# A RetNet attention stage and a PReLU MLP in one kernel: the first part's decays moved into its mask, into k and into q's copy, other unread products on the matrix engine, and another order of creation

## The chip, the cores and the metric

The kernel runs on one core of a Trainium2 chip. The time is that of the device in microseconds (us), the median over several executions; lower is better. Besides, one execution was taken by the hardware profiler, and everything that is read out of a profile or a trace below comes from that one execution.

The engines are named as the profile names them: PE multiplies matrices (PEld is its loading of the stationary operand), DVE and ACT work elementwise and read the accumulators, POOL works elementwise but not on the accumulators, SP issues the transfers (DMA).

## What is computed

```python
def _attn_ref(q, k, v):                      # 8 x 8 heads x 576 x 64 each
    scores = scale * np.matmul(q, k.transpose(0, 1, 3, 2))
    gamma = 1.0 - 2.0 ** (-5.0 - np.arange(H))
    rel = pos[:, None] - pos[None, :]
    Dmat = np.where(rel >= 0, gamma[:, None, None] ** rel[None, :, :], 0.0)
    return np.matmul(scores * Dmat, v)

def _moe_ref(x, w_in, w_out, alpha):         # x: 4608 x 512, d_ff 2048
    h = x @ w_in
    g = np.maximum(h, 0.0) + alpha * np.minimum(h, 0.0)
    return g @ w_out
```

x is the attention's output, with the 8 heads of a token side by side. All inputs and the output are float32.

## The kernel before

**Attention in chunks.** The 576 positions of a head are 9 chunks of 64. Within a chunk the scores are masked and multiplied into v; from chunk to chunk a state (k transposed times v, with its decay) is carried. For the first two batches this is done in six *parts* (`PARTS`): part x is batch x // 3, and chunks 0-3, 4-7 or 8, for all heads at once. `load_part` loads k, q and v of a part (256 KB each time that it is called for one m, two m per tensor); `part_transposes(x, i)` turns k (i = 0) or q (i = 1) on PE and ACT copies it out; `part_scale(x, i)` multiplies q (i = 1) or v (i = 2) on POOL by a table of decays `tp`, so that the decay between two positions comes out of the product of two factors; `part_scores`, `part_states` and `part_values` are the products of 64 x 64; the scores are masked on DVE, `part_carry` hands the state on by POOL; ACT copies the result into x. `last_part` does parts 2 and 5 (one chunk). Later batches go through `joint`, two heads at a time, whose operands come by their own loads (`load_kq`, `load_kn`, `load_v`), by `operands` and by round trips through DMA.

**The MLP.** The 4608 tokens are 18 blocks of 256. Eight `cells`, a block with two of the sixteen slices of d_ff each, are done first and plainly (`unit_plain` makes h, `second_plain` multiplies by w_out); they use the weights as 32 pieces, loaded and rebuilt one by one by `weights` / `convert`: two operations on ACT, three on DVE, one on POOL (L754), in this order. One piece is 512 KB. Cell 0 (block 0, slice 0) needs pieces 0 and 1 for its two halves of `unit_plain` and 2 and 3 for the two products of each half m of `second_plain`; cell 1 (block 0, slice 1) needs 4 and 5, then 6 and 7. Everything after that goes with operands split into three parts (`split_w`, `split_roll`, `unit_roll`, `second`).

**What sets the order.** Every operation is recorded with `do(engine, cost, function, reads, writes)`; the creation order decides which operation waits for which when they share a buffer, and which bank of the accumulators each gets. Then `dues` and `plan` put all recorded operations in an order by a table of costs written in the kernel, a random search changes the due times, and the order with the smallest planned total is written out. So each engine gets one fixed sequence, and it executes that sequence in order: an instruction that waits holds up all those behind it on its engine. Loads all go through SP's queue; in the first part of the run a load waits until at most 1.25 MB are under way (`IN_FLIGHT`). `fill(n, cost)` records n products of 128 x 128 that nothing reads (18 in all: 5, 3 and 10). `tables` makes small tables of decays, on DVE (L393 to L403).

**The first steps** stand at the end of the function: loads of part 0, `fill(5)`, k's transposes, `fill(3)`, q scaled and transposed, the scores, v scaled, three pieces of weights, the states, `tables`, the values, `fill(10)`, then part 1 between the cells, and so on up to `split_w`; then a loop over s makes the rest.

Of the kernel before, what the change touches and what calls it, by code (L numbers as in the profile page):

```python
# [10 lines left out]
FP32 = mybir.dt.float32  # L11
# [6 lines left out]
ALU = mybir.AluOpType  # L18
# [3 lines left out]
def kernel(  # L22
# [120 lines left out]

    gch = const.tile([P, 3, NPAIR], FP32, name="gch")
# [34 lines left out]
    def do(eng, cost, fn, r=(), w=(), late=0.0, lock=False, kind=None, hold=0.0, size=0):  # L179
# [19 lines left out]
        op.deps = [d for d in deps if d is not op]  # L199
# [145 lines left out]
    EARLY, JOINTS = 1, {(s, i): 1 for s in range(14) for i in range(2) if (s, i) not in ((0, 0), (8, 1), (10, 1), (13, 0), (13, 1))}  # L345
# [46 lines left out]
    def tables():  # L392
        nc.vector.reciprocal(pf[:, 1], pf[:, 1])  # L393
        nc.vector.tensor_tensor(out=th[:, 1], in0=pf[:, 1], in1=th[:, 2], op=ALU.mult)
        for h2 in range(2):
            hd = slice(h2 * D, (h2 + 1) * D)
            nc.vector.tensor_copy(tabk[half(1 - h2)], th[half(1 - h2), 1, h2:H:2])
            nc.vector.tensor_copy(gch[hd, 0], th[hd, 2, h2:H:2])
            nc.vector.tensor_scalar(tabx[hd, :, 0], pf[hd, 0, h2:H:2], QSCALE, None, ALU.mult)
            nc.vector.scalar_tensor_tensor(out=tabx[hd, :, 1], in0=dif[hd, 5, h2:H:2], scalar=1.0,  # L400
                                           in1=tabx[hd, :, 0], op0=ALU.add, op1=ALU.mult)
        for i in range(2):
            ins = nc.vector.tensor_tensor(out=gch[:, i + 1], in0=gch[:, i], in1=gch[:, i],  # L403
                                          op=ALU.mult)
        return ins


# [41 lines left out]
    def part_scale(x, i):  # L449
        j0, j1 = PARTS[x % 3]  # L450
        rows = min(P, (j1 - j0) * C)
        for m in range((j1 - j0 + 1) // 2):
            def f(m=m):
                t = part(x, i)[0:rows, m]
                return nc.gpsimd.tensor_tensor(
                    out=t, in0=t, in1=tp[0:rows, i - 1, m, :, None].to_broadcast([rows, H, D]),
                    op=ALU.mult)
            do("POOL", 1.05, f, (), [key_p(x, i, m)], lock=True)
# [8 lines left out]
    def part_transposes(x, i, bank):  # L467
# [6 lines left out]
        for m in range(2):  # L474
# [9 lines left out]
            def g(m=m, pt=pt):  # L484
                nc.scalar.copy(at()[:, :, m * P:(m + 1) * P],
                               pt.get().rearrange("p (c s) -> p c s", c=NPAIR))
            do("ACT", 0.59, g, [(pt, 0)], [(t, "t", m)])

    def part_scores(x, bank):
# [18 lines left out]
        for h2 in range(2):  # L508
            def g(h2=h2):
# [3 lines left out]
                    in1=mask[:, None, :].to_broadcast([P, 8, C]), op=ALU.mult)  # L513
            do("DVE", 0.69, g, [(ps[h2], 0), (ps[h2], 1)], [(a, "m", h2)])
# [892 lines left out]

    def of_pe():
        return [op for op in ops if op.eng == "PE"][-1:]

    load_part(0, ((0, 0), (1, 0), (1, 1), (0, 1), (2, 0), (2, 1)))
    bank = banks_of(0)
    fill(5, 0.43)
    part_transposes(0, 0, bank)
    fill(3, 0.43, [next(op for op in ops if op.eng == "PE" and len(op.deps))])
    part_scale(0, 1)
    part_transposes(0, 1, bank)
    part_scores(0, bank)
    part_scale(0, 2)
    weights(3)  # L1420
    part_states(0, bank)
    do("DVE", 2.0, tables, (), [(cst, "t")])
    part_carry(0)
    part_values(0, bank)
    fill(10, 0.25, of_pe())
    weights(1)
    fetch_x(visits[0])
    dma(lambda: a16, lambda: moe_alpha.rearrange("(t p) -> t p", p=P), NFC * P * 4, (), [(cst, "al")])
    aps = Gen(psa[0])
    do("PE", 0.2, lambda: nc.tensor.transpose(aps.get()[:, 0:NFC], a16, ident[0:NFC, 0:NFC]), [(cst, "al")],  # L1430
       [(aps, 0)])
    do("DVE", 0.1, lambda: nc.vector.tensor_scalar(malpha, aps.get()[:, 0:NFC], -1.0, 1.0,
                                                   ALU.mult, ALU.add), [(aps, 0)], [(cst, "a")])
    load_part(1)
    bank = banks_of(1)
    unit_plain(cells[0])
    weights(2)
    part_transposes(1, 0, bank)
    part_scale(1, 1)
    part_transposes(1, 1, bank)  # L1440
    second_plain(cells[0])
    weights(2)
    part_scale(1, 2)
    part_scores(1, bank)
    part_states(1, bank)
    unit_plain(cells[1])
    load_part(2)
    part_values(1, bank)
    part_carry(1)
    fetch_x(visits[1])  # L1450
    part_scale(2, 1)
    part_scale(2, 2)
    rooms(3)
    load_part(3)
    second_plain(cells[1])
    unit_plain(cells[2])
    last_part(2)
    weights(2)
    for x in (4, 5):
        rooms(x)  # L1460
    part_transposes(3, 0, bank)
    part_scale(3, 1)
    part_transposes(3, 1, bank)
    second_plain(cells[2])
    part_scores(3, bank)
    part_scale(3, 2)
    part_states(3, bank)
    part_carry(3)
    unit_plain(cells[3])
    part_values(3, bank)  # L1470
    load_part(4)
    weights(2)
    second_plain(cells[3])
    part_transposes(4, 0, bank)
    part_scale(4, 1)
    part_transposes(4, 1, bank)
    unit_plain(cells[4])
    load_part(5)
    weights(2)
    second_plain(cells[4])  # L1480
    part_scores(4, bank)
    part_scale(4, 2)
    part_states(4, bank)
    part_carry(4)
    unit_plain(cells[5])
    part_values(4, bank)
    load_kq(8)
    load_kn(8)
    load_v(8)
    weights(2)  # L1490
    second_plain(cells[5])
    part_scale(5, 1)
    part_scale(5, 2)
    unit_plain(cells[6])
    last_part(5)
    operands(8)
    load_kq(9)
    load_v(9)
    second_plain(cells[6])
    unit_plain(cells[7])  # L1500
    done.add(8)
    joint_(8)
    second_plain(cells[7])
    for i in range(16):
        split_w(i)

    ready_kb = [((kb + 1) * TB - 1) // S for kb in range(NKB)]
    todo = iter(range(2 * NPAIR + 1, len(pairs) + 1))
# [103 lines left out]
    was_in = lxs[0].gen.ops + lxs[1].gen.ops  # L1612
    lxs[:] = lx_slots("x")
    for x in lxs:
        Gen(x).before = was_in
    for _ in range(EARLY):
        joint_(next(todo))
    land[0] = LAND[1]
    split_roll(visits[2])
    last = singles - 1  # L1620
    t = 8
    for s in range(last):
# [3 lines left out]
        queue += [now_cells[vis["n"], u] for vis in some for u in us]  # L1626
        quick[0] = s >= QUICK
        by_side = sorted(some, key=lambda vis: vis["kb"] % 2)
        if s == 0:
            split_roll(visits[3])  # L1630
        for i, u in enumerate(us):
            cs = [now_cells[vis["n"], u] for vis in by_side]
            gens, g = take_rooms(cs)
            for f in range(2):
                for _ in range(ahead.get(t, 0)):
                    convert((op_, 0), was, None)
                t += 1
                ps = unit_roll(by_side, u, f, True)
                acts_roll(ps, gens, g, u, f)
                if f:  # L1640
                    for c, ga in zip(cs, gens):
                        c["ga"] = ga, ga.get
                    ahead_g()
# [104 lines left out]
```

## Time and profile before

| | us |
|---|---|
| median of 3 runs | 919.32 |
| lowest and highest of them | 918.11, 922.28 |
| profiled execution, its span | 917.4 |
| PE busy in it | 906.9 (99%) |
| DVE, ACT, POOL busy | 548.0, 503.9, 520.2 |

The span is the time from the first to the last instruction; the median of the runs lies 1.9 us above the span of the profiled execution. A row of the timeline gives start, duration, engine, line, operation, output and inputs, shapes, how many instructions are drawn together, and in brackets the engine's idle time before it with what ended it. "issue" stands where nothing in the profile is seen to have been waited for. A matmul's end is modelled, so a row can reach a little into the next one.

### The profile page before, as it was taken

What the parts mean: (1) busy time and instruction counts of PE and PEld (TensorE: products, weight loads), DVE (VectorE), ACT (ScalarE), POOL (GpSimd) and SP (SyncE); (2) the same over time, 40 slices, a digit from 0 to 9 for tenths busy, and PEclk for the clock granted to TensorE, in tenths of its full rate; (3) what the DMA queues carried; (4) which work ended last, traced back from release to release, by engine and by line L of the source; (5) the groups of instructions that cost most, each with busy time, mean ns of one, the idle gap of its engine ahead of it and who ended that gap; (6) DMA issues with size and microseconds to landing.
All of it is one profiled execution on the core that took longest, in us unless ns stands there. A gap on an engine that the chain in (4) does not pass through costs nothing. (4 is left out here: it accounts for less than half of the span.)

```text
span 917.4 us, 19097 instructions
## 1 busy us (share of the span) xinstructions
PE 906.9 (99%) x7289; PEld 737.8 (80%) x7289; DVE 548.0 (60%) x1003; ACT 503.9 (55%) x1010; POOL 520.2 (57%) x461
## 2 busy tenths in 40 slices
PE   7999999999999999999999999999999999999998
PEld 6767688887888888888888888888888888888886
DVE  5786766667677667676757776344444534344343
ACT  4575455646565656565746555537463636364441
POOL 4776746456466665674542244665656656574624
PEclk9999999999999999999999999999999999999999
DMA  9995688977988879895243332212121322211112
GB/s 216 251 235 86 164 189 186 198 178 155 221 192 194 209 166 201 193 189 181 93 138 130 102 125 65 86 57 81 58 89 56 99 73 86 74 64 47 47 46 69
DMA packets 235947, 121.32 MB, mean 132 GB/s; under 512 B 203456, under 2 KB 203728, under 8 KB 235856
## 3 DMA queue, kind: packets, MB, share of 16 engines
q1 hardware_dynamic: 235712, 119.98, 52.1%
q8 instruction: 57, 0.93, 0.4%
q14 instruction: 34, 0.28, 0.1%
q10 hardware_dynamic: 144, 0.13, 0.0%
HBM read 74.19 MB, written 32.51 MB: 116 GB/s over the span
## 5 line engine op out<-in xcount | busy, mean ns | idle before, releaser
L1340 PE MATMUL pso<-w,g 128*128 128x512 f32 x1392 | 338.8, 391 | 0.0
L1340 PEld LDWEIGHTS pso<-w,g 128*128 128x128 f32 x1392 | 258.9, 188 | 55.2 <-POOL g L1267 1.2
L1264 POOL TENSOR_TENSOR g<-ga_all,g 128x512 fp32r<-128x512 f32 x76 | 97.9, 1291 | 130.4 <-ACT g L1260 105.0
L1267 POOL TENSOR_TENSOR g<-g 128x512 fp32r<-128x512 f32 x114 | 147.4, 1294 | 23.7 <-DVE su L1066 5.7
L1188 PE MATMUL psh<-lx_x,w 128*128 128x512 f32 (+1 forms) x360 | 86.6, 379 | 0.0
L1188 PE MATMUL psa<-lx_x,w 128*128 128x512 f32 (+1 forms) x360 | 85.4, 376 | 0.0
L1188 PEld LDWEIGHTS psa<-lx_x,w 128*128 128x128 f32 x360 | 65.1, 188 | 13.1 <-issue 0.4
L1188 PEld LDWEIGHTS psh<-lx_x,w 128*128 128x128 f32 x360 | 64.2, 188 | 12.9
L1260 ACT ACTIVATE g<-ga_all 128x512 fp32r<-128x512 f32 x76 | 47.6, 631 | 43.0 <-PE pso L1340 21.0
L1256 POOL TENSOR_TENSOR g<-g 128x512 fp32r<-128x512 f32 x22 | 28.5, 1296 | 64.0 <-DVE g L1253 38.3
L1264 POOL TENSOR_TENSOR g<-vn,g 128x512 fp32r<-128x512 f32 x25 | 32.4, 1297 | 37.5 <-ACT g L1260 34.9
L1340 PE MATMUL pso<-lx_x,g 128*128 128x512 f32 x216 | 53.5, 390 | 0.1
L1163 POOL TENSOR_TENSOR lx_x<-lx_x 128x512 fp32r<-128x512 f32 x28 | 35.9, 1294 | 26.0 <-DVE lx_x L1160 26.0
L941 DVE SCALAR_TENSOR_TENSOR at<-psa,pf,mask 64x512 f32<-64x512 f32 x48 | 36.0, 749 | 21.1 <-PE psh L861 10.2
L1340 PEld LDWEIGHTS pso<-lx_x,g 128*128 128x128 f32 x216 | 40.4, 188 | 9.0 <-DVE o L1363 0.7
L1262 ACT ACTIVATE g<-ga_all 128x512 fp32r<-128x512 f32 x76 | 47.2, 621 | 0.0
L1358 DVE TENSOR_TENSOR op<-pso,op 128x512 f32<-128x512 f32 x35 | 24.0, 686 | 31.3 <-PE pso L1340 31.2
L1202 ACT COPY ga_all<-psh 128x512 f32<-128x512 f32 (+1 forms) x30 | 16.7, 558 | 39.1 <-PE psh L1188 37.4
L861 PEld LDWEIGHTS psh<-at,vn 128*64 128x64 f32 x864 | 27.9, 137 | 8.7 <-issue 3.6
L1222 PE MATMUL psh<-w,w 128*128 128x512 f32 x144 | 34.6, 389 | 0.0
L1222 PE MATMUL psa<-w,w 128*128 128x512 f32 x144 | 34.6, 389 | 0.0
L754 POOL TENSOR_TENSOR wa<-wa,op 128x512 int32<-128x512 int32 x16 | 21.0, 1311 | 23.1 <-DVE wa L751 19.1
(329 smaller groups left out, 1883.3 us busy)
## 6 DMA issues: line engine op xcount, KB each, us to landing
xk<-x SPq DMA_DIRECT2D x18, 512.0 KB, 3.7
ok<-o SPq DMA_DIRECT2D x36, 256.0 KB, 2.9
op<-ok SPq DMA_DIRECT2D x18, 512.0 KB, 3.9
out_dram<-o SPq DMA_DIRECT2D x35, 256.0 KB, 2.3
x<-xk SPq DMA_DIRECT2D x16, 512.0 KB, 5.6
qx<-in_q_dram SPq DMA_DIRECT2D x96, 72.0 KB, 3.4
kx<-in_k_dram SPq DMA_DIRECT2D x96, 72.0 KB, 3.3
kn<-in_k_dram SPq DMA_DIRECT2D x48, 144.0 KB, 3.4
```

The costliest lines, as they stand in the source:

```text
L861: nc.tensor.matmul(pv[i].get()[half(h2), (j - js[0]) * C:(j - js[0] + 1) * C], vns[n % 2][:, h2, j], mt.get()[:, h2, j], start=True, stop= ...
L941: nc.vector.scalar_tensor_tensor(out=mt.get()[half(1 - h2), h2, j], in0=fro[x], scalar=pf[x, 1, h:h + 1], in1=mask[x, None, :].to_broadcas ...
L1163: do("POOL", 1.29, lambda h=h, l=l, d=d: nc.gpsimd.tensor_tensor(out=piece(d()), in0=h(), in1=l(), op=ALU.subtract), [(g, 0, n), (g, 1, n) ...
L1188: nc.tensor.matmul(out_of(p), w[:, c0:c0 + P], xp(l, cc), start=(l != 1 and cc == 0), stop=(l > 0 and cc == NCC - 1))
L1222: nc.tensor.matmul(p.get(), w[:, c0:c0 + P], piece(words_of(g)[:, o:o + DM]), start=(l != 1 and cc == 0), stop=(l > 0 and cc == NCC - 1))
L1256: do("POOL", 1.29, lambda: nc.gpsimd.tensor_tensor(out=piece(to.get()[:, 2]), in0=to.get()[:, 0], in1=to.get()[:, 1], op=ALU.subtract), [( ...
L1260: do("ACT", 0.64, lambda: nc.scalar.mul(piece(to.get()[:, 2]), whole(), BELOW), both, [(to, 2)])
L1262: do("ACT", 0.64, lambda: nc.scalar.mul(piece(to.get()[:, 0]), whole(), BELOW * 2.0 ** -12), both, [(to, 0)])
L1264: do("POOL", 1.29, lambda: nc.gpsimd.tensor_tensor(out=piece(to.get()[:, 1]), in0=whole(), in1=to.get()[:, 2], op=ALU.subtract), both + [( ...
L1267: do("POOL", 1.29, lambda: nc.gpsimd.tensor_tensor(out=piece(to.get()[:, 2]), in0=to.get()[:, 0], in1=to.get()[:, 1], op=ALU.subtract), [( ...
L1340: nc.tensor.matmul(a[2 * m + b].get(), piece(g.get()[:, l, f, m * P:(m + 1) * P]), w_piece(u, 2 + f, l), start=(cell["first"] and f == 0 a ...
L1358: do("DVE", 0.69, lambda: nc.vector.tensor_tensor(out=t(), in0=p1.get(), in1=t(), op=ALU.subtract), [(p1, 0)], [tk])
```

## The change

**Part 0.** Its q and v are no longer scaled on POOL. k is scaled in place by POOL instead (`part_scale(0, 0)`, with the table that v had), after its transposes have read it, for the states alone; the transposed k and v stay as they were loaded. q's decays go into the copy that takes its transposes out of the accumulators: ACT's copy becomes a DVE multiplication with a table `rise`, one for each m. The mask of the scores becomes a table `fade` (mask times the same decays), made by two POOL operations of 128 x 512. `rise` is made on DVE, by doubling: four small operations and a memset, then eight multiplications that get longer. Other parts are done as before.

**Tables.** One reciprocal is moved ahead of the recorded operations; `tables` goes from DVE to POOL, as 13 small operations in place of 11.

**Unread products.** Of the 18 products of 128 x 128 two stay, and five groups of 16 products of 64 x 64 (`small_fill`) are added.

**Order.** The recorded operations up to s = 3 of the loop are created in the order of a list `early`, in which loads, parts, pieces of weights, cells, splits, joints and the first units of the split MLP are interleaved differently; the rest of the loop starts at s = 4. Dependencies of an operation are sorted by number. The products of the program stay the same but for the unread ones.

```diff
+    nc.vector.reciprocal(pf[:, 1], pf[:, 1])
...
-        op.deps = [d for d in deps if d is not op]
+        op.deps = sorted((d for d in deps if d is not op), key=lambda d: d.n)
...
-    EARLY, JOINTS = 1, {(s, i): 1 for s in range(14) for i in range(2) if (s, i) not in ((0, 0), (8, 1), (10, 1), (13, 0), (13, 1))}
+    FIRST, JOINTS = 4, {(s, i): 1 for s in range(14) for i in range(2) if (s, i) not in ((0, 0), (8, 1), (10, 1), (13, 0), (13, 1))}
...
     def tables():
-        nc.vector.reciprocal(pf[:, 1], pf[:, 1])
-        nc.vector.tensor_tensor(out=th[:, 1], in0=pf[:, 1], in1=th[:, 2], op=ALU.mult)
+        nc.gpsimd.tensor_tensor(out=th[:, 1], in0=pf[:, 1], in1=th[:, 2], op=ALU.mult)
         for h2 in range(2):
             hd = slice(h2 * D, (h2 + 1) * D)
-            nc.vector.tensor_copy(tabk[half(1 - h2)], th[half(1 - h2), 1, h2:H:2])
-            nc.vector.tensor_copy(gch[hd, 0], th[hd, 2, h2:H:2])
-            nc.vector.tensor_scalar(tabx[hd, :, 0], pf[hd, 0, h2:H:2], QSCALE, None, ALU.mult)
-            nc.vector.scalar_tensor_tensor(out=tabx[hd, :, 1], in0=dif[hd, 5, h2:H:2], scalar=1.0,
-                                           in1=tabx[hd, :, 0], op0=ALU.add, op1=ALU.mult)
+            nc.gpsimd.tensor_copy(tabk[half(1 - h2)], th[half(1 - h2), 1, h2:H:2])
+            nc.gpsimd.tensor_copy(gch[hd, 0], th[hd, 2, h2:H:2])
+            nc.gpsimd.tensor_scalar(tabx[hd, :, 0], pf[hd, 0, h2:H:2], QSCALE, None, ALU.mult)
+            nc.gpsimd.tensor_scalar(tabx[hd, :, 1], dif[hd, 5, h2:H:2], 1.0, None, ALU.add)
+            nc.gpsimd.tensor_tensor(out=tabx[hd, :, 1], in0=tabx[hd, :, 1], in1=tabx[hd, :, 0],
+                                    op=ALU.mult)
         for i in range(2):
-            ins = nc.vector.tensor_tensor(out=gch[:, i + 1], in0=gch[:, i], in1=gch[:, i],
+            ins = nc.gpsimd.tensor_tensor(out=gch[:, i + 1], in0=gch[:, i], in1=gch[:, i],
                                           op=ALU.mult)
         return ins
+
+    rise, fade = Gen(gs[2]), Gen(op_)
+    powers = const.tile([P, NBIT + 1, NPAIR], FP32, name="powers")
+
+    def rise_of():
+        return words_of(rise)[:, 0:1024].rearrange("p (c s) -> p c s", c=NPAIR)
+
+    def fade_of(h2):
+        return words_of(fade)[:, h2 * DM:(h2 + 1) * DM]
+
+    def rises():
+        for h2 in range(2):
+            hd = half(h2)
+            nc.vector.tensor_scalar(powers[hd, 0:NBIT], dif[hd, :, h2:H:2], 1.0, None, ALU.add)
+            nc.vector.tensor_copy(powers[hd, NBIT], th[hd, 0, h2:H:2])
+        t = rise_of()
+        nc.vector.memset(t[:, :, 0:1], QSCALE)
+        for i in range(NBIT):
+            ins = rise_by(i)
+        return ins
+
+    def rise_by(i):
+        n, t = 1 << i, rise_of()
+        return nc.vector.tensor_tensor(
+            out=t[:, :, n:2 * n], in0=t[:, :, 0:n],
+            in1=powers[:, i, :, None].to_broadcast([P, NPAIR, n]), op=ALU.mult)
+
+    def fades(h2):
+        return nc.gpsimd.tensor_tensor(
+            out=fade_of(h2).rearrange("p (c m s) -> p c m s", c=NPAIR, m=2),
+            in0=mask[:, None, None, :].to_broadcast([P, NPAIR, 2, C]),
+            in1=tp[:, 1].rearrange("p m (c h) -> p c m h", h=2)[:, :, :, h2:h2 + 1].to_broadcast(
+                [P, NPAIR, 2, C]), op=ALU.mult)
+
+    def first_tables():
+        do("DVE", 1.6, rises, (), [(rise, 0)])
+        do("DVE", 0.69, lambda: rise_by(NBIT), [(rise, 0)], [(rise, 1)])
+        for h2 in range(2):
+            do("POOL", 1.3, lambda h2=h2: fades(h2), (), [(fade, h2)], lock=True)
...
     def part_scale(x, i):
+        i_t = i or 2
         j0, j1 = PARTS[x % 3]
         rows = min(P, (j1 - j0) * C)
         for m in range((j1 - j0 + 1) // 2):
             def f(m=m):
                 t = part(x, i)[0:rows, m]
                 return nc.gpsimd.tensor_tensor(
-                    out=t, in0=t, in1=tp[0:rows, i - 1, m, :, None].to_broadcast([rows, H, D]),
+                    out=t, in0=t, in1=tp[0:rows, i_t - 1, m, :, None].to_broadcast([rows, H, D]),
                     op=ALU.mult)
             do("POOL", 1.05, f, (), [key_p(x, i, m)], lock=True)
             do("PE", 0.52 if x else 0.65, f, [key_p(x, i, m)], [(pt, 0)], size=8)
             def g(m=m, pt=pt):
-                nc.scalar.copy(at()[:, :, m * P:(m + 1) * P],
-                               pt.get().rearrange("p (c s) -> p c s", c=NPAIR))
-            do("ACT", 0.59, g, [(pt, 0)], [(t, "t", m)])
+                to, fro = at()[:, :, m * P:(m + 1) * P], pt.get().rearrange("p (c s) -> p c s", c=NPAIR)
+                if x or not i:
+                    nc.scalar.copy(to, fro)
+                else:
+                    nc.vector.tensor_tensor(out=to, in0=fro, in1=rise_of()[:, :, m * P:(m + 1) * P],
+                                            op=ALU.mult)
+            if x or not i:
+                do("ACT", 0.59, g, [(pt, 0)], [(t, "t", m)])
+            else:
+                do("DVE", 0.69, g, [(pt, 0), (rise, m)], [(t, "t", m)])
     def part_scores(x, bank):
         a = Gen((gs[1], ats)[x // 3]) if x % 3 == 0 else room[x + 1, 2]
                 nc.vector.tensor_tensor(
                     out=at()[:, h2].rearrange("p (n s) -> p n s", s=C),
                     in0=ps[h2].get().rearrange("p (n s) -> p n s", s=C),
-                    in1=mask[:, None, :].to_broadcast([P, 8, C]), op=ALU.mult)
-            do("DVE", 0.69, g, [(ps[h2], 0), (ps[h2], 1)], [(a, "m", h2)])
+                    in1=mask[:, None, :].to_broadcast([P, 8, C]) if x else
+                    fade_of(h2).rearrange("p (n s) -> p n s", s=C), op=ALU.mult)
+            do("DVE", 0.69, g, [(ps[h2], 0), (ps[h2], 1)] + ([] if x else [(fade, h2)]),
+               [(a, "m", h2)])
     def part_states(x, bank):
         pu = [Gen(next(bank)) for _ in range(2)]
...
+    def small_fill(after=()):
+        def f():
+            for n in range(16):
+                a = half(n % 2)
+                nc.tensor.matmul(unread.get()[a, 0:C], ident[a, 0:C], ident[a, 0:C], start=True,
+                                 stop=True)
+        do("PE", 0.58, f, (), [(unread, 0)], kind="small", size=64).deps.extend(after)
+
...
-    load_part(0, ((0, 0), (1, 0), (1, 1), (0, 1), (2, 0), (2, 1)))
-    bank = banks_of(0)
-    fill(5, 0.43)
-    part_transposes(0, 0, bank)
-    fill(3, 0.43, [next(op for op in ops if op.eng == "PE" and len(op.deps))])
-    part_scale(0, 1)
-    part_transposes(0, 1, bank)
-    part_scores(0, bank)
-    part_scale(0, 2)
-    weights(3)
-    part_states(0, bank)
-    do("DVE", 2.0, tables, (), [(cst, "t")])
-    part_carry(0)
-    part_values(0, bank)
-    fill(10, 0.25, of_pe())
-    weights(1)
-    fetch_x(visits[0])
-    dma(lambda: a16, lambda: moe_alpha.rearrange("(t p) -> t p", p=P), NFC * P * 4, (), [(cst, "al")])
...
+    early = (
+        lambda: load_part(0, ((0, 0), (1, 0), (1, 1), (0, 1), (2, 0), (2, 1))),
+        lambda: part_transposes(0, 0, bank0),
+        lambda: small_fill(),
+        lambda: first_tables(),
+        lambda: weights(1),
+        lambda: load_part(2),
+        lambda: small_fill(),
+        lambda: alpha(),
+        lambda: weights(1),
+        lambda: part_scale(0, 0),
+        lambda: load_kq(8),
+        lambda: weights(1),
+        lambda: fill(2, 0.43),
+        lambda: load_part(1),
+        lambda: small_fill(of_pe()),
+        lambda: weights(1),
+        lambda: weights(1),
+        lambda: part_transposes(0, 1, bank0),
+        lambda: do("POOL", 3.0, tables, (), [(cst, "t")], lock=True),
+        lambda: small_fill(of_pe()),
+        lambda: weights(1),
+        lambda: part_states(0, bank0),
+        lambda: part_scale(1, 1),
+        lambda: part_scores(0, bank0),
+        lambda: part_transposes(1, 1, bank1),
+        lambda: part_transposes(1, 0, bank1),
+        lambda: part_scale(2, 1),
+        lambda: small_fill(of_pe()),
+        lambda: weights(1),
+        lambda: part_scores(1, bank1),
+        lambda: part_carry(0),
+        lambda: part_values(0, bank0),
+        lambda: fetch_x(visits[0]),
+        lambda: rooms(3),
+        lambda: unit_plain(cells[0]),
+        lambda: part_scale(1, 2),
+        lambda: weights(1),
+        lambda: second_plain(cells[0]),
+        lambda: load_part(3),
+        lambda: part_scale(2, 2),
+        lambda: part_states(1, bank1),
+        lambda: unit_plain(cells[1]),
+        lambda: part_scale(3, 2),
+        lambda: part_values(1, bank1),
+        lambda: load_kn(8),
+        lambda: part_carry(1),
+        lambda: part_scale(3, 1),
+        lambda: rooms(4),
+        lambda: weights(1),
+        lambda: last_part(2),
+        lambda: weights(1),
+        lambda: part_transposes(3, 1, bank1),
+        lambda: fetch_x(visits[1]),
+        lambda: unit_plain(cells[2]),
+        lambda: load_part(4),
+        lambda: weights(1),
+        lambda: second_plain(cells[1]),
+        lambda: rooms(5),
...
+    for step in early:
+        step()
+    land[0] = LAND[1]
+    for s in range(FIRST, last):
+        begin(s)
+        for i in range(2):
             for f in range(2):
-                for _ in range(ahead.get(t, 0)):
-                    convert((op_, 0), was, None)
-                t += 1
-                ps = unit_roll(by_side, u, f, True)
-                acts_roll(ps, gens, g, u, f)
-                if f:
-                    for c, ga in zip(cs, gens):
-                        c["ga"] = ga, ga.get
-                    ahead_g()
+                unit(s, i, f)
                 pump(PUMP_R[i][f])
-                if f:
-                    for _ in range(JOINTS.get((s, i), 0)):
-                        joint_(next(todo))
-                if i and f and 3 + s <= last and s:
-                    assert NPAIR * (ready_kb[3 + s] + 1) in done
-                    split_roll(visits[3 + s])
+            for _ in range(JOINTS.get((s, i), 0)):
+                next_joint()
+        if 3 + s <= last:
+            next_split(3 + s)
```

## The prediction

> **What bounds the kernel now.** I read the busy time by stretch first: ten stretches of 10 us from the start. Columns: stretch, length, then busy time of PE, PEld, DVE, ACT, POOL with counts, granted clock, share of the DMA engines, GB/s.
>
> ```profile
> 0.00:10.00 10.00, 7.19 (x44) 6.12 (x48) 6.33 (x41) 3.16 (x5) 4.81 (x18) 1.00 0.92 175
> 10.00:20.00 10.00, 8.30 (x315) 7.30 (x308) 4.36 (x10) 3.99 (x8) 4.15 (x5) 1.00 1.05 252
> 20.00:30.00 10.00, 9.03 (x221) 7.41 (x219) 9.30 (x16) 6.55 (x12) 6.46 (x6) 1.00 0.88 237
> 30.00:40.00 10.00, 9.23 (x109) 6.11 (x110) 7.99 (x14) 6.27 (x12) 8.11 (x7) 1.00 1.06 241
> 40.00:50.00 10.00, 10.00 (x151) 7.61 (x150) 5.94 (x11) 5.62 (x11) 6.07 (x6) 1.00 1.05 257
> ```
>
> PE idles 2.81 + 1.70 + 0.97 + 0.77 = 6.25 us in the first 40 us, of 917.4 - 906.9 = 10.5 us in the whole span; from then on it is full, and the DMA engines are full over the first 80 us (shares 0.88 to 1.06). So the run is PE's work plus what PE loses at the start, and the start is fed by loads. The list of PE's waits and its timeline say where:
>
> ```profile
> PE psa L599 <- ACT spy L588: 1.0, 1, 1.0
> ...
> PE psh L861 <- DMA vn<-su: 0.2, 1, 0.2
> ```
>
> ```profile
> 15.86 0.34 PE L574 MATMUL pso<-g,w 64*64 64x64 f32 x7 [1.32 <-issue]
> ...
> 18.97 2.61 PE L1405 MATMUL psh<-ident 128*128 128x128 f32 x20
> ```
>
> The last row is `fill(10)`: busy, but nothing reads it. PE's last idle time in the first 40 us is at 31.57; from 32.12, where cell 0's `second_plain` begins, everything is useful and without a gap. POOL's timeline shows what arrives when, since it waits for loads in order:
>
> ```profile
> 12.71 1.04 POOL L455 TENSOR_TENSOR w<-w,tp 128x512 f32<-128x512 f32 x1 [1.23 <-DMA w<-in_q_dram]
> ...
> 20.75 1.04 POOL L455 TENSOR_TENSOR w<-w,tp 128x512 f32<-128x512 f32 x1 [2.87 <-DMA w<-in_v_dram]
> ...
> 30.09 1.04 POOL L455 TENSOR_TENSOR w<-w,tp 64x512 f32<-64x512 f32 x1 [1.23 <-DMA w<-in_q_dram]
> 31.10 1.28 POOL L754 TENSOR_TENSOR lx_w<-lx_w,w 128x512 int32<-128x512 int32 x1
> ...
> 35.07 1.04 POOL L455 TENSOR_TENSOR w<-w,tp 64x512 f32<-64x512 f32 x1 [0.57 <-DMA w<-in_v_dram]
> 36.07 1.28 POOL L754 TENSOR_TENSOR lx_w<-lx_w,w 128x512 int32<-128x512 int32 x1
> ```
>
> Counted in tiles of 256 KB in SP's order, these are landings of tile 8 (q of part 1) at 12.71, 15 at 20.75, 22.5 at 30.09 and 27.5 (v of part 2) at 35.07. The line through them: tile n lands at 3.0 + 1.17 n. I use it for the changed order. The two L754 rows finish weight pieces 3 (32.38) and 5 (37.35), each held behind the scale of a load.
>
> **The change, part by part.** PE's useful products are the same in number and form (I counted them in the instruction orders of both kernels), and changes between kinds of product are as frequent. So the time changes only by what PE loses before it is full, and by any new hole later.
>
> *Unread products.* Removed: `fill(10)`, 2.55 us up to the next product at 21.51. It hid a wait: after it come 1 us of part 1's scores, then PE idles 0.43 us for piece 0, which POOL finishes at 21.75 + 1.30 = 23.05. Alone its removal buys nothing past 23.1. The first fills (2.50 and 1.28 us, before 6.4) stood while k was loading; their successors stand there too. Two groups of 64x64 come later, before the second half of part 0's scores and before cell 0; 16 such products take 0.58 us or less in the rows of L503 (0.56 for 10.52 to 11.08), and both stand where PE waits anyway. Value 0; 1.2 us in all if the cover is gone.
>
> *Part 0.* SP's new order is k, v, q of part 0 (tiles 2, 4, 6), q of part 1 (8), piece 0 (10), k of part 1 (12), piece 1 (14), v of part 1 with piece 2 between (15, 18), piece 3 (20), piece 4 (22), q of part 2 (22.5), piece 5 (24.5), then as before up to v of part 2 (27.5). POOL: k's tables are ready at 5.5 (L142), so k's scales and the two `fade` operations run 5.6 to 10.2 (twice 1.04 and 1.29: L455, L754). The 13 small operations of `tables` have no row on POOL; between 0.15 (its 128x64 memset) and 0.29 (its 128x128 select) each, 2.0 to 3.8 us; they are nearer the small end but depend on each other, so 3.0: done 13.2, and part 1's q scaled at 15.3. DVE: the setup ends 5.6; `rise` is 13 operations, the short ones 0.2 apart as in L393 to L403, the longest 0.69: done near 9. PE: states 9.5 (their second half waits for k's second scale, 8.9), q's transposes 10.8 (q lands 8.9 and 10.0), DVE's two copies with `rise` 12.9 (0.69 each, among four sums of 0.42), scores 13.5, masks 14.9, then transposes and values to 18.0, 1.39 for the L615 products: 19.4. Before, these ended at 18.5: 0.9 us later now, with no effect, for cell 0 and v of part 1 come later still.
>
> *Part 1 and cell 0.* Scores to 20.5; x's three copies by ACT (0.59) to 21.2; first half of cell 0 (1.86) to 23.1; v's second half is tile 18 instead of 16, lands 24.1, scaled 25.1, states to 25.7; second half 27.6; values 1.1; the `spy` copy, priced at its wait, 1.0; 1.2 for the rest: PE reaches `second_plain` of cell 0 at 30.9, before at 32.1. That is 1.2 us ahead, most of the removed fill.
>
> *The gates.* Now PE runs into pieces 3 and 5, which the change leaves where they were: the same bytes are ahead of q and v of part 2 (tiles 22.5 and 27.5), and POOL still has their scales ahead of L754's successor. Piece 3 is done at 32.4, piece 5 at 37.4. From 30.9: first product of half m = 0 to 31.9, the second waits to 32.4 and ends 33.3; part 2's transposes 0.7: 34.0; cell 1's first half 35.9; part 2's scores 36.4; then PE waits 1.0 us for piece 5. Before, 37.4 found PE busy for 5.3 us since 32.1: both halves m of cell 0 (3.7), transposes 0.7, and 0.9 of cell 1's first half. Now, half m = 1 (1.86) is put after piece 5's products. Done by 37.4 before but not now: 1.86; now but not before: the other 0.95 of cell 1's half and 0.5 of scores. Net +0.4 us. The 1.2 us gained are lost waiting, and the order after it is a little worse.
>
> *Later.* Past 37.4 I cost the reordering at 0. Cover: two blocks' work per piece, so the pieces come faster than PE uses them; the next gates are piece 7 (landing 39.9, behind v of part 3, near 44.6; used at 47.4) and the joint's k (tile 61 with its smaller packets: near 80; used near 84). If a cover fails, the stall goes through 1:1, as nothing behind has a hole to fill: 6.25 of the 10.5 idle us are in the first 40, and the chain at the end (last 137 PE rows) has the same order in both.
>
> Sum: 917.4 + 0.4 = 917.8 for the profiled execution; on the median, 919.32 + 0.4, 919.7. Ends of its terms: -1.0 if piece 5 is ready when PE comes, +1.6 if the later unread products and `tables` at 3.8 lie open: 918.3 to 921.3 on the median.
>
> [...] k's four transposes at 4.17 and 6.36 take 1.12 and 1.06 us, q's at 8.11 0.66, with a granted clock of 1.00 throughout. [...]
>
> **The rivals.**
>
> *Joints starve (slower).* Between 100 and 280 us the DMA engines are 0.76 to 0.90 busy while PE is full, and the one wait there is that of L861 for vn<-su, 0.2 us at 221: the joints' round trips (3.5 us landing) just meet PE. If the new order puts a joint's loads behind more others, PE stands at each `values`. Eight joints lie in the moved stretch; from 0.35 us each it passes 0.5%; at 0.7 it is 5.6: 917.8 + 5.6 = 923.4, 925.3 on the median. Against: sizes and number of the loads are unchanged.
>
> *The start closes up (faster).* If loads land several us sooner, the gates go. Idle after the first wait in 40 us is 6.25 - 1.7 = 4.6, `fill(10)` 2.55: 7.1 at most, 912.2 on the median. For: share 0.88 from 20 to 30. Against: 1.05 and 1.06 beside it.
>
> [...]
>
> *It does nothing* falls together with the forecast.
>
> **How the numbers follow.** Forecast 0.55, joints 0.22, closing up 0.13, slow array 0.10. A change within 0.5% (914.7 to 923.9) is about what a measurement of this kernel can't tell from none. Faster: the closing up, 0.13. Same: the forecast and most of the slow array, 0.64. Slower: joints and the rest, 0.23. The range reaches towards both outer cases, 914.0 to 925.5; the forecast's own is 918.3 to 921.3.
>
> **What would show it.** Right: PE reaches cell 0's `second_plain` near 31, waits there or at cell 1's second half for POOL's last operation on a piece, that one preceded by a wait for v of part 2 near 35; no idle PE afterwards. Wrong: v of part 2 landing before 33 or after 37; PE idle at `values` or joints after 80 us; transposes of over 1 us past 9 us; a first stage in which PE reaches piece 5 after 38.

## The result, and the profile after

The changed kernel takes 925.04 us (median of 4 runs, 923.29 to 927.84), the kernel before 919.57 beside it (4 runs, 918.11 to 922.28). The ratio is 1.0061, with a 95% interval from 1.0036 to 1.0086: 3.3 to 7.9 us slower. The profiled execution of the changed kernel has a span of 926.1 us, 8.7 more than the one before; it is the longest of the four (spans of the others: 921.6, 922.1, 924.6).

Busy time by stretch of the changed kernel (columns as before: PE, PEld, DVE, ACT, POOL with counts, granted clock, DMA share, GB/s):

```profile
0.00:10.00 10.00, 6.69 (x113) 6.06 (x113) 8.19 (x41) 2.46 (x3) 5.63 (x19) 1.00 0.95 177
10.00:20.00 10.00, 8.16 (x208) 7.13 (x208) 7.12 (x14) 1.93 (x4) 6.32 (x17) 0.83 1.08 250
20.00:30.00 10.00, 9.09 (x306) 7.72 (x305) 7.02 (x12) 7.44 (x13) 5.90 (x5) 1.00 0.93 249
30.00:40.00 10.00, 6.14 (x135) 4.26 (x134) 7.63 (x14) 4.33 (x9) 6.97 (x7) 0.78 0.99 221
40.00:50.00 10.00, 10.00 (x95) 6.39 (x94) 5.42 (x10) 3.76 (x7) 4.73 (x5) 0.88 0.83 204
```

PE idles 9.92 us in the first 40 us, before 6.25, and the granted clock, 1.00 in all of these stretches before, falls to 0.83, 0.78 and 0.88. Its list of waits (who waited for whom, total, times, longest) names the places:

```profile
PE psh L649 <- issue: 3.3, 1, 3.3
PE psa L576 <- DVE malpha L1474: 2.9, 1, 2.9
...
PE psh L551 <- issue: 0.8, 1, 0.8
...
PE psh L911 <- ACT w L833: 0.6, 1, 0.6
```

And PE's timeline, rows of the changed kernel around the two long ones:

```profile
8.06 0.33 PE L576 MATMUL pso<-w,w 64*64 64x64 f32 x4
11.27 0.27 PE L576 MATMUL psa<-w,w 64*64 64x64 f32 x2 [2.88 <-DVE malpha L1474]
...
33.64 0.23 PE L649 MATMUL psa<-w,w 64*64 64x64 f32 x2
37.18 0.37 PE L649 MATMUL psh<-w,w 64*64 64x64 f32 x2 [3.32 <-issue]
...
38.23 3.78 PE L1172 MATMUL pso<-lx_w,ga_all 128*128 128x512 f32 x4
```

The last row is the first half of cell 0's `second_plain`. It starts at 38.23 (before 32.12) and takes 3.78 us (before 1.98), at half rate (granted clock 0.50 over these 3.78 us, 1.00 over the 1.98). So the 8.7 us fall into three: 6.1 up to that half, 1.8 in it, and 0.8 in all that follows. Of the waits listed past 45 us the changed kernel has four that add to 1.4 us (0.6 at L911, 0.4 at L624), the one before two that add to 0.4.

The first wait has its cause on DVE (start, duration, then engine, line, operation) and POOL beside it:

```profile
6.14 4.99 DVE L431 TENSOR_TENSOR g<-g,powers 128x4 f32<-128x4 f32 x7
11.05 0.17 DVE L1474 TENSOR_SCALAR malpha<-psa 128x16 f32<-128x16 f32 x1
11.17 0.69 DVE L431 TENSOR_TENSOR g<-g,powers 128x512 f32<-128x512 f32 x1
```

```profile
7.45 1.06 POOL L436 TENSOR_TENSOR op<-mask,tp 128x512 f32<-128x512 f32 x1
8.47 1.04 POOL L496 TENSOR_TENSOR w<-w,tp 128x512 f32<-128x512 f32 x1
9.47 1.06 POOL L436 TENSOR_TENSOR op<-mask,tp 128x512 f32<-128x512 f32 x1
```

Alpha's transpose (done at 8.13) and part 0's states share the bank psa[0]; the states may start when DVE has read alpha out. DVE reads it behind seven doublings, which take 4.99 us: the third to the sixth end just behind POOL's operations, one by one, at about 1.0 us each in place of 0.17 to 0.29 (their times in the run with alpha's bank below, where they are through before POOL starts).

### The profile page after: what moved, and what is told of

Read it like the earlier page. It is cut to its first block, busy times and chain, and to the rows that moved or that the text cites. A ratio compares the mean times of both kernels' runs of the same rounds, so it can differ in the third digit from the quotient of the medians.

```text
span 926.1 us, 19395 instructions
## 1 busy us (share of the span) xinstructions
PE 910.9 (98%) x7417; PEld 740.5 (80%) x7417; DVE 552.4 (60%) x1007; ACT 501.9 (54%) x1008; POOL 523.1 (56%) x474
## 5 line engine op out<-in xcount | busy, mean ns | idle before, releaser
L1213 POOL TENSOR_TENSOR lx_x<-lx_x 128x512 fp32r<-128x512 f32 x28 | 35.9, 1292 | 33.6 <-DVE lx_x L1210 31.0
L1314 POOL TENSOR_TENSOR g<-vn,g 128x512 fp32r<-128x512 f32 x25 | 32.4, 1295 | 39.7 <-ACT g L1310 36.7
L911 PEld LDWEIGHTS psh<-at,vn 128*64 128x64 f32 x864 | 27.7, 137 | 8.8 <-issue 4.6
```

What stands on the lines that cost most here:

```text
L911: nc.tensor.matmul(pv[i].get()[half(h2), (j - js[0]) * C:(j - js[0] + 1) * C], vns[n % 2][:, h2, j], mt.get()[:, h2, j], start=True, stop= ...
L1213: do("POOL", 1.29, lambda h=h, l=l, d=d: nc.gpsimd.tensor_tensor(out=piece(d()), in0=h(), in1=l(), op=ALU.subtract), [(g, 0, n), (g, 1, n) ...
L1314: do("POOL", 1.29, lambda: nc.gpsimd.tensor_tensor(out=piece(to.get()[:, 1]), in0=whole(), in1=to.get()[:, 2], op=ALU.subtract), both + [( ...
```

## How PE's program comes

The "issue" wait in L649 names nobody. The DMA view of the changed kernel over 29 to 34.3 us and then over 34.3 to 36 us (busy tenths in 40 slices; queue, kind: packets, MB, share):

```profile
DMA  2199997576699997999699999999999999999999
...
## 3 DMA queue, kind: packets, MB, share of 16 engines
q1 hardware_dynamic: 2642, 1.17, 108.2%
```

```profile
DMA  9894434323333221000000000009900790302249
...
## 3 DMA queue, kind: packets, MB, share of 16 engines
q1 hardware_dynamic: 215, 0.14, 46.3%
q8 instruction: 1, 0.02, 4.7%
```

For more than five microseconds the engines moved only loads (q1), with hardly a gap. Then, as these ran out, one packet of 16,384 bytes came on q8, from 34.39 to 35.67, and PE went on at 37.18. The page counts 58 such packets in the run. Loads of weights, multiplications and PE's waits for semaphores counted together, PE's stalls for "issue" come after 961 and 1473 instructions in the changed kernel, 512 apart, and after 450 and 1217 in the one before, 767 apart, one short of three times 256; in the first experiment below after 961, 1217 and 1473, 256 apart. So I count in stretches of 256 PE instructions from these places and call such a stretch a block; it is some 127 products, each a load and a multiplication. The lists of PE's waits of the fourteen kernels traced here hold 24 waits for "issue" of over 0.2 us, these seven among them. In the first 40 us of the two kernels eleven packets came on q8, each after PE had passed the end of a block: 1.2 to 3.1 us later in the kernel before, 1.1 to 5.8 in the changed one. That such a packet is the block after the one that PE has just begun, I read from this order in time; no run shows it directly.

| kernel | PE passes the end before | packet starts, takes | PE stands at the next end, goes on |
|---|---|---|---|
| before | 25.7 | 28.75, 1.27 | 0.28 (L599), 31.57 |
| changed | 28.6 | 34.39, 1.28 | 3.32 (L649), 37.18 |

From the packet's end to PE's next product it is 1.5 us in both. So from the end of the block before to the product that PE stands for it is in these two cases 2.8 us plus the time until the packet starts, 5.8 us here and 3.0 before. That this time is a queue behind loads is my reading of the engines being full meanwhile (q1's share is 108.2% from 29 to 34.3 us). One case speaks against it: in the kernel with part 0 alone (below) a packet started only 4.9 us after PE had passed the end (25.54 to 30.40), though the DMA engines were 10% busy. In part 0 and part 1, where products of 64x64 follow each other every 0.02 us, a block is through in 2.5 to 5.0 us (the changed kernel passes block ends at 15.6, 20.5 and 23.0, goes on at 24.0, and passes the next at 28.6 and 33.6).

## The experiments

Three theories went in. A: the doubling beside POOL, alpha's bank and the clock that falls after the wait. B: PE stands for its program, once more than before because of the five small groups (each of their 80 products is two in the trace, so 320 instructions, less 64 of the 16 products removed: one block). C: the later order.

**The start of part 0, taken apart.** First the table `rise` is filled by two memsets (its contents, and so the output, are not the reference's):

```diff
-        nc.vector.memset(t[:, :, 0:1], QSCALE)
-        for i in range(NBIT):
-            ins = rise_by(i)
-        return ins
+        return nc.vector.memset(t, QSCALE)
...
-        do("DVE", 0.69, lambda: rise_by(NBIT), [(rise, 0)], [(rise, 1)])
+        do("DVE", 0.69, lambda: nc.vector.memset(rise_of()[:, :, P:2 * P], QSCALE), [(rise, 0)], [(rise, 1)])
```

> Left out: the doublings of q's table (the table is filled by two memsets), so the output is not the reference's. All other rows and their order are those of the changed kernel. Theory A (the table's doublings collide with POOL's operations, 1.0 us a step instead of 0.2, hold malpha's read and with it the bank of part 0's states, and PE's 2.9 us wait then halves its clock): the 2.9 us wait and the half-rate stretch near 11.8 us go, PE reaches cell 0's second_plain 2 to 4 us earlier, median 921 to 923. Theory B (the loss is the 3.3 us instruction wait at L649 and the half rate after it): that wait stays, median 923 to 925. Theory C (the loss lies in the order after 80 us): 925, as the changed kernel.

924.81 us (10 runs; ratio 1.0056, 1.0037 to 1.0075). The wait for alpha is gone, but PE then stands in the later places:

```profile
PE psh L646 <- issue: 3.3, 1, 3.3
...
PE psh L548 <- issue: 1.6, 1, 1.6
```

`second_plain` starts at 37.12, 1.1 us earlier, and the median is 0.2 lower. The doubling alone is not the loss.

Then alpha's transpose gets the bank psa[1]:

```diff
         aps = Gen(psa[0])
+        aps.get = lambda got=[]: got[0] if got else got.append(psa[1].make()) or got[0]
```

> Only the bank of alpha's transposed copy is changed, so that part 0's states needn't wait for malpha's read; same order. Theory A, bank alone: PE's 2.9 us wait at the states goes, but q's table still ends near 11.9 and holds the sums and q's copies, so PE waits a little later instead; 0 to 1 us gained, median 924 to 925; the half-rate stretch may move rather than go. If the bank were all of it: 2.9 plus 1.7 of half rate, 920 to 921.

924.36 us (1.0049, 1.0030 to 1.0069; runs from 921.42 to 926.50). The profiled execution is a lucky one: span 919.7, clock 1.00, `second_plain` at 33.35. In it the packet came 1.2 us after PE passed the end, and there is no stall in L649. Besides, POOL's first scale of k starts at 7.52 (changed kernel: 6.45), behind six of the doublings, so that q's table ends at 10.31 and not near 11.9 as expected: the good start is not the bank's alone. Same program, 5.1 us between its runs: the time until one packet starts, 1.2 or 5.8 us, would account for most of that.

**Fewer instructions.** The last two small groups left out:

```diff
+    groups = []
...
-            for n in range(16):
+            groups.append(0)
+            for n in range(16 if len(groups) < 4 else 0):
```

> The two later groups of unread products of 64x64 (in the middle of part 0's scores, and before cell 0) are left out, 128 PE instructions fewer; same order otherwise. Theory B (instruction blocks of 256 run out inside a run of small products): the end of the block moves from part 1's L649 products to wider ones, the 3.3 us wait and the half-rate stretch from 35.7 us go, the 0.8 us wait in part 1's scores stays or grows to 2; median 920 to 922. Theory A alone: only the fills' own 1.2 us at most, 924 to 925.

923.47 us (1.0042, 1.0020 to 1.0064), above the 920 to 922 of theory B and within the noise of the changed kernel. L649 is free, but the block end in part 1's scores now costs 2.8 us (0.8 in the changed kernel):

```profile
PE psh L551 <- issue: 2.8, 1, 2.8
PE psa L576 <- DVE malpha L1477: 2.6, 1, 2.6
```

Then all small groups out, with three products of 128x128 each in place of the second and third (not of the first two, as the expectation has it, and 296 PE instructions fewer in the trace, not 312):

```diff
+    groups = []
...
-            for n in range(16):
-                a = half(n % 2)
-                nc.tensor.matmul(unread.get()[a, 0:C], ident[a, 0:C], ident[a, 0:C], start=True,
-                                 stop=True)
+            groups.append(0)
+            for _ in range((0, 3, 3, 0, 0)[len(groups) - 1]):
+                nc.tensor.matmul(unread.get()[:, 0:P], ident, ident, start=True, stop=True)
```

> The changed kernel with other unread products: none of the five small groups of 64x64; their first two become three products of 128x128 each, the others are left out (312 PE instructions fewer, counting loads; the order of everything else is unchanged). Theory B (PE stands because the next 16 KB of its program comes late; the five small groups push one more such block in front of cell 0's second_plain): no 'issue' wait of over 1 us inside L649, second_plain starts before 36 us, at most one short half-rate stretch after 12 us, median 920.5 to 922.5. Rival A (rise on DVE beside POOL, the states waiting for alpha's bank): the wait of the states stays at 2.9 us, median 924 to 925. Rival C (the order later in the run): 924 to 925.

927.02 us (1.0092, 1.0075 to 1.0109): no better than the changed kernel (1.0036 to 1.0086), against theory B as I had put it. One block fewer, but its end lies in L649 again, twenty products further, and PE stands there for 2.3 us; besides it waits 4.1 us for alpha and runs at half rate until 15.7 (granted clock 0.71 from 10 to 20 us). So fewer blocks are not enough while an end lies there.

On top of this the bank, and `rise` made on DVE ahead of the tables `tp`, which move behind it:

```diff
...
+    rises()
+    rise_by(NBIT)
+    nc.vector.tensor_tensor(out=tp[:, 0, 1], in0=tp[:, 0, 0], in1=th[:, 0], op=ALU.mult)
+    nc.vector.reciprocal(tp[:, 1], tp[:, 0])
...
```

> As the kernel with a block fewer, and besides alpha's transpose has another bank than part 0's states, and rise is made on DVE ahead of the recorded operations. A and B together: no wait of the states, no stall in L649, second_plain before 34 us, clock 1.00 nearly throughout, median 918 to 920.5. C (the order later in the run costs the time): 923 or more although the first 40 us are mended.

926.76 us (1.0087, 1.0072 to 1.0102). Not mended: POOL now waits for DVE and scales k 2.4 us later (8.80 for 6.45), and the states stand for that (4.2 us in two waits). The stall at the block end of the last run is there too (2.2 us in L644, its L649).

The bank, the six products, and four unread products of 128x128 behind alpha's transpose:

```diff
...
+        def turn():
+            ins = nc.tensor.transpose(aps.get()[:, 0:NFC], a16, ident[0:NFC, 0:NFC])
+            for _ in range(4):
+                nc.tensor.matmul(unread.get()[:, 0:P], ident, ident, start=True, stop=True)
+            return ins
...
```

> The changed kernel with alpha's transpose in another bank than part 0's states, without small groups (one left out, two replaced by three products of 128x128 each, the last two left out), and with four products of 128x128 behind alpha's transpose, where PE waits for k's scale on POOL. If the start is lost to that bank and to the clock: the states end before 10.5 us, granted clock 1.00 from 10 to 20 us, second_plain of cell 0 between 32.5 and 35 us, median 919.5 to 922.5. If what comes later than the first stage costs the time: 924 or more although second_plain begins before 34.

928.48 us (1.0101, 1.0073 to 1.0129). The states end at 9.58, as expected. Then DVE is late: the doublings beside POOL last until 11.9, q's copies come behind them, and PE waits 3.3 us for `g`; in L649 it stands as before.

```profile
PE psa L649 <- issue: 3.4, 1, 3.4
PE pso L551 <- DVE g L530: 3.3, 2, 2.7
```

**Less loading at a time.** At most 0.75 MB of loads under way in place of 1.25:

```diff
-    LIMITED, IN_FLIGHT = 100.0, 5 << 18
+    LIMITED, IN_FLIGHT = 100.0, 3 << 18
```

> Only the limit on bytes under way in the first part is changed, 0.75 MB instead of 1.25 MB; same order. Theory B: an instruction fetch queues behind fewer bytes, so the 3.3 us wait at L649 shrinks to under 1.5; median 921 to 924. Rival (the start is fed by loads, so fewer under way slows them): v of part 2 lands 1 to 3 us later than 37.1, median 926 to 929.

931.59 us (1.0135, 1.0090 to 1.0180), above both expectations, but the packets come sooner: all six in the first 40 us start 0.9 to 2.3 us after PE has passed the end before, and L649 has no "issue" wait. With 1.25 MB the same six in the changed kernel took 1.1 to 5.8. The loads themselves are slower for it, as the rival had it (DMA share 0.70 and 0.78 from 10 to 30 us, 1.08 and 0.93 in the changed kernel; POOL scales v of part 2 from 40.44, there from 37.13), which costs more than the stalls.

**The kernel before, with other unread products ahead of cell 0.** Three variants of one place: 64 of 64x64 for the ten of 128x128 (64 for the 10 in the second line of the diff); none (only the last two lines); ten of 64x64 (as shown).

```diff
-            for _ in range(n):
+            for m in range(10 if n == 10 else 0):
+                a = half(m % 2)
+                nc.tensor.matmul(unread.get()[a, 0:C], ident[a, 0:C], ident[a, 0:C], start=True,
+                                 stop=True)
+            for _ in range(n if n < 10 else 0):
                 nc.tensor.matmul(unread.get()[:, 0:P], ident, ident, start=True, stop=True)
```

> The kernel before with its ten unread products of 128x128 ahead of cell 0 replaced by 64 of 64x64 (216 more PE instructions, about the same busy time). Theory B: one more block of instructions has to come before cell 0's second_plain; PE stands one time more for 'issue', 1 to 4 us, and the median is 920.5 to 924. Rivals A and C, for which the number of unread instructions is nothing: 919 to 919.7, no change.

> The kernel before without its ten unread products of 128x128 (2.55 us busy). The prediction's account of this removal (it hides a wait for piece 0 and buys nothing past it): PE reaches cell 0 earlier and waits for piece 0 to 23.1 us, median 918.5 to 919.5. If it does cover nothing: 916.5 to 917.5. If PE's clock needs it: half rate from about 20 us, median 921 to 923.

> The kernel before with its ten unread products of 128x128 ahead of cell 0 replaced by ten of 64x64: as many PE instructions, so the 256-instruction blocks of PE's program end at the same products as before; about 2.2 us less busy time. If the loss of 2.7 us in the kernel without them came from where the blocks end: no 'issue' stall of over 0.5 us in L599, median 916.8 to 919.5. If it came from the missing busy time itself (PE arrives sooner, before the blocks and pieces are there, and stands): 920.5 to 922.5, with stalls of over 1 us in L599 and a wait for piece 0.

64 small: 922.90 us (1.0050, 1.0028 to 1.0072). None: 921.74 (1.0030, 1.0018 to 1.0043). Ten small: 918.85 (0.9997, 0.9985 to 1.0010). Each of the ten is in the trace two products, as is each of the 64, so ten small ones leave the block ends where they were and the two others move them by the same twenty products (108 more are a block, 128, less twenty). These two stand in L599; the wait in L574 lies ahead of the place of the edit, so that its 1.3 to 2.2 us in these kernels are not the edit's:

```profile
PE psa L599 <- issue: 2.5, 1, 2.5
PE pso L574 <- issue: 2.2, 1, 2.2
PE psh L1091 <- POOL lx_w L754: 2.0, 1, 2.0
```

```profile
PE pso L574 <- issue: 1.9, 1, 1.9
...
PE psa L599 <- issue: 1.4, 1, 1.4
```

The first of these fences is the kernel with none, the second that with 64. With ten small ones L599 has no such wait, only L574 (1.4; before 1.3) and the ten themselves (0.8):

```profile
PE pso L574 <- issue: 1.4, 1, 1.4
...
PE psh L1091 <- POOL lx_w L754: 1.2, 1, 1.2
PE psh L1406 <- issue: 0.8, 1, 0.8
```

To take 2.2 us of unread work out is worth nothing (0.3 us, within the interval); to take it out and let twenty products move up against the block ends costs 2.9 (921.74 - 918.85).

**Parts alone.** The kernel before with the new part 0 and the tables on POOL; and the changed kernel with the old part 0. Both are planned anew, so much of their order differs.

```diff
...
-    part_scale(0, 1)
+    part_scale(0, 0)
+    first_tables()
...
-    part_scale(0, 2)
...
-    do("DVE", 2.0, tables, (), [(cst, "t")])
+    do("POOL", 3.0, tables, (), [(cst, "t")], lock=True)
```

```diff
...
-        lambda: first_tables(),
...
-        lambda: part_scale(0, 0),
+        lambda: part_scale(0, 1),
...
+        lambda: part_scale(0, 2),
-        lambda: do("POOL", 3.0, tables, (), [(cst, "t")], lock=True),
+        lambda: do("DVE", 2.0, tables, (), [(cst, "t")]),
```

> The kernel before with the new part 0 alone (k scaled, q's copy by rise, fade, tables on POOL); creation order and unread products as before, the order of all operations planned anew. The prediction's account (part 0 costs nothing at the end): 919 to 920.5. If part 0's new operations on DVE and POOL make the loss: 922 to 926, with q's transposes and the scores of part 0 waiting for DVE or POOL.

> The changed kernel with part 0 as before (q and v scaled on POOL, the ACT copy, the plain mask, tables on DVE); creation order and unread products as changed, the order of all operations planned anew. If the order and the small products make the loss: 923 to 927. If part 0 makes it: 918.5 to 921.

The first: 930.54 us (1.0130, 1.0099 to 1.0161). The two longest waits of PE:

```profile
PE pso L553 <- ACT lx_w L784: 4.4, 1, 4.4
PE psh L913 <- DVE ga_all L1255: 2.4, 1, 2.4
```

The first is of part 0's scores. The list names ACT's operation on a piece of weights, which ended then too, but the scores read k's copies, which ACT had done by 7.83, and q's copies by DVE, the first of them done at 12.48:

```profile
6.99 4.89 DVE L432 TENSOR_TENSOR g<-g,powers 128x4 f32<-128x4 f32 x8
11.80 1.28 DVE L532 TENSOR_TENSOR g<-pso,g 128x512 f32<-128x512 f32 x2
```

So the scores wait for the doublings, as the second expectation has it. That the whole loss comes from there is not shown: `second_plain` starts at 29.80, sooner than in the kernel before (32.12), and what follows takes 899.4 us in place of 885.3, in an order planned anew.

The second: 925.92 us (1.0066, 1.0037 to 1.0095), as much as the whole change. So the loss does not need the new part 0. Its profiled execution (span 921.4, clock 1.00) has 2.6 us of "issue" waits before `second_plain`, which starts at 33.84; from there to the end it takes 887.6 us, the kernel before 885.3. The two kernels in the changed order that do this product at full rate (alpha's bank, the last two groups left out) take 886.3 and 886.4. Theory C has some part in it, about 1 us in that order.

## Why the prediction missed the side

The time lies inside the range (914.0 to 925.5), near its upper end, and outside the forecast's own (918.3 to 921.3). That the range holds it is luck: its upper end was drawn from the joints' rival, and the joints did not starve. Two slips of the working change nothing here: from 919.7 the lower end of the forecast's own would be 918.7, and eight joints pass 0.5% from nearly 0.6 us each, not 0.35. By the prediction's steps:

*`rise`, "done near 9".* 11.86. The sum took the short operations at 0.2 us each, from a stretch of DVE ahead of POOL's first long operation (6.99); beside POOL's operations of 128x512 they take about 1.0. Even the trace before shows one (0.89 us, the second of L403). The `fade` operations took 1.06 (sum: 1.29) and the 13 small ones 3.9 (sum: 3.0, bound 3.8).

*Part 0, "0.9 us later now, with no effect".* The states end at 12.88 (sum: 9.5), since the wait for alpha's bank was not in the sum at all; part 0 ends at 22.74 (sum: 19.4). That this 3.3 us has little effect at the end is nearly right, but not for the reason given: the two kernels without this wait gain 0.2 and 0.7 us in the median, less than their intervals can tell; in the first PE only came earlier to its missing instructions.

*"PE reaches `second_plain` of cell 0 at 30.9".* 38.23. This is the step that failed: 3.3 us of it from part 0, 4.1 from two stalls for instructions (0.8 in L551, 3.3 in L649). The sum had waits for loads, POOL, DVE and ACT, and none for the arrival of PE's program, though two rows before the change said "issue" (1.32 in L574, 0.28 in L599). I left them as they were.

*Unread products, "value 0".* Right for their busy time (the ten small ones: no change), wrong for their number: 20 products up or down are 2.9 us on the kernel before. "1.2 us in all if the cover is gone" bounded the wrong quantity.

*The gates.* Pieces 3 and 5 are done at 34.47 and 39.4 (sum: 32.4 and 37.4), 2 us late with v of part 2. PE came later still and waited for neither.

*Later, "costed at 0".* 0.8 us in this execution by the three-part sum; idle PE past 80 us was named as a sign against the forecast, and 0.4 us (L624) and 0.6 us (L911) of it came. PE reaching piece 5 after 38 was another, and came.

*The rivals.* Joints starving: L911, which is L861 of the kernel before, waits once for 0.6 us, not in eight joints. The start closing up: no. The slow array, which has 0.10 of the chances: no run shows that term. What the changed kernel showed is half rate from 11.76 to 15.17 and 35.65 to 42.48, the first time behind 2.88 us of idle PE (8.39 to 11.27), the second within 3.32 (33.86 to 37.18). Behind its first unread products (64 of 64x64 from 1.70 to 5.23, four of 128x128 to 5.87) k's transposes took 0.60 and 0.66 us; before, behind ten products of 128x128, 1.12 and 1.06 (the clock's records begin at 7.30 there, so its 1.00 does not cover them). The first stretch cost the eight transposes of part 0's q 0.65 us (1.97 for 1.32), the second 1.8 us.

What stays open: that moved block ends give the changed kernel its time back was not tried. In the changed kernel every edit that took products out also moved the ends to another place with short products, so the share of the stalls in the 5.5 us rests on one execution with the stall (926.1) and one nearly equal one without (919.7, alpha's bank and POOL's start apart). Why one packet starts 1.2 us after PE has passed the end of a block and another 5.8, in the same order of loads, is not settled either; no run beat the kernel before.

## What to carry to other kernels

A wait for "issue" in the profile of before need not stay where it is or as short as it is: in L599 it was 0.28 us, in L649, the same line of the changed kernel, 3.32. Count the instructions of the engine between two such waits, here 512 and 767, and see what the change does to their number and place. Tiny unread products cost instructions even where their time is free (the kernel before takes 2.9 us longer with none of the ten than with ten small ones); where fillers are taken out or put in, keep the number of instructions the same or look where the blocks end. And a wait that is mended at the start is worth only what the next gate lets through: here two kernels without a wait of 2.9 us gained less than 1 us.

## What the runs showed of the hardware

In the first 40 us of the two kernels the eleven packets of 16,384 bytes on q8 started 1.1 to 5.8 us after PE had passed the end of a block of 256 instructions, with up to 1.25 MB of loads under way. They took 0.95 to 1.62 us. At the four places where PE stood for "issue" (before L574 and L599, in the changed kernel L551 and L649) it went on 1.29 to 1.55 us after a packet's end.

The changed kernel's half-rate stretches last 3.41 and 6.83 us, the stretch at full rate between them 20.48, six times 3.41. In the kernel before the longest idle time of PE from 7.30 us on is 1.32, and the clock stays at 1.00. The kernel before without the ten waits for "issue" for 2.2 us in L574 and 2.5 in L599; its granted clock is 0.83 from 10 to 20 us, where the first lies, and 1.00 from 30 to 40, where the second lies. How much idle time lowers the clock, and how it has to lie, these runs do not settle.
